# DFT over m and output projection in one-bank operations of 512 elements, in a re-searched order

## The chip, the cores and the metric

The program runs on one core of a Trainium2 chip. Its time is the device time of one execution in microseconds. The kernel before took 454.33 us (median of three runs, 454.22 to 454.91). The profile was taken on a further execution of 453.94 us, whose span from the first to the last instruction is 452.2 us.

Names used below: PE is the matrix engine, PEld its weight loads, DVE the vector engine, ACT the scalar engine, POOL the engine that cannot read PSUM, SP the queue that issues the transfers. PSUM is the memory that PE writes; it has eight banks of 512 fp32 numbers per partition here.

## What is computed

Four sequences of 6272 steps with 256 channels go through a gated recurrence and then through a gated long convolution:

```python
f = lower_bound + (1 - lower_bound) * sigmoid(f_logit)
h[t] = f[t] * h[t-1] + (1 - f[t]) * x[t]                 # recurrence, x becomes h
x1, x2, x3 = split(h @ w_proj)                           # 256 -> 3 * 256
conv = irfft(rfft(x2, n=S) * rfft(filter_fft, n=S), n=S) # over the sequence, S = 6272
out = (x1 * conv * x3) @ w_out
```

## The kernel before

The sequence is written as 6272 = 128 x 49, and the Fourier transform over it is done as small matrix products in two steps: one over m (128 values) and one over r (49 values). For each of the four batches there are these operations, each a short run of instructions recorded by `op` (L78) with what it reads and writes:

- `hgrn` (L342): 13 chunks. Loads of f_logit and x, a sigmoid on ACT ("sig"), a product on POOL ("u"), transposes on PE ("su", L374), the gate ("f", L387 on ACT or L389 on DVE) and the recurrence as a scan on DVE (L395). ("wrap" copies a part of h on POOL.)
- `gate` (L410): "x13" on PE (L423), one bank each; its results leave PSUM as "xs" copies on ACT or DVE, or as a product on DVE (L444); the rest of the products ("z") are on POOL (L453).
- `phase_p` (L720): the projection of x2, 13 operations "P" on PE (L729), with evictions "x2" of 1024 elements. P needs all scans of its batch.
- `phase_f1` (L737): the DFT over m. 16 operations "F1" of eight matmuls (L742), each into two banks, and each with one eviction "A" of 1024 elements into the buffer A, which has four slots of eight pairs.
- `unit` (L788): the DFT over r ("F2", L804), the product with the filter's spectrum (on DVE straight from PSUM, L827; or an ACT or DVE copy of 512 elements and then a POOL product, L836), the inverse over r ("I2", L846) and its eviction "Th" (784 elements).
- `phase_o` (L896): 13 groups of four rows (the last has one). "I1" (L909, two banks), the product "y" on DVE (L915) into one of two `ys` buffers, the output projection "proj" (L927: eight matmuls into two banks), one eviction "o" of 1024 elements into a staging buffer (`osb`, `PP` or `HA`, by `places`, L893), and one store. The first y of a batch needs all of the batch's I2 results and gate products.

A "y" begins only when its batch's spectrum is done; meanwhile the next batch's `hgrn` runs. So a batch has a first stretch (P, F1, F2, I2, x13, and some scans of the next batch) and a second one (I1, y, proj, o, and the last scans of the next batch).

The order of all of this is fixed in the kernel: `ORDER` (L126) is a text in which three characters give one operation, the engine that does it and its first PSUM bank. `emit` (L109) writes the operations out in this order, so that every engine has its own fixed queue. An operation that may run on two engines has its engine from there too ("MUL" is DVE's product straight from PSUM). `copy` (L286) writes an eviction for the engine it is given; the page shows these under L289 and L291 (ACT), L294 and L296 (DVE).

The buffer marks that set the dependences are `At` (L268, one mark for a slot of A), `Ax` (L272) and `place_t` (L887, the marks of a staging buffer).

Of the kernel before, what the change touches and what calls it, by code (L numbers as in the profile page):

```python
# [62 lines left out]
class Plan:  # L63
# [67 lines left out]
    "QD/WCPSERACSACQCD9MCNUEHQCOECUSEAOEBOCYWEcgEzgEngEogEIIEJIE0gELUE9gCVCCMYCTYESYCZGE1ACaSCbCCfWCgGEMMENMChQCiIETSEpAE"
    "eYCcYCjYEqYCdWEXUCeGCoQEYEEUKEVKCkWEZMCpAClGEfSE/ACvQCqUEjWEgKCwIEhKCrEEkGCxQErUCyIElOCtSFHgAGgFJAEvQEsEEtME+gCWgFIg"
    "FRgCuCAHgFSgFbgC4WEwAExIEKYE2YCsYAIYAJYAKYCzYE3SFAYC6UC5GE4CC7EFKYC8YAMYC0WE5KE6QC1GC/UE7IDBSFTADAMDCCE8IFBWC9UFESFC"
    "GC+EFDOFFCCHgFcgFlgB3gFmgFvgFwgDIQDJADKUDLEDEWDFGALIEWYAOYDDYDMYFUYDyYFLQFOUFGKFPEDPSFMIFNIDQCFdAFQMDaWDNSDOCDbGFeYA"
    "NYFVQFYUFZEFnAFWIFXIDRSJSWJTXFfQJUGDSCJVHFxAFaMJXWFiSFgIJZOFhIFjCDUUDVEFkKFoYFpWDhQEmYDTYEiYEuYFyYD2YEOYECYEaYD+YFsU"
    "DfSFqGFrODiADYQFtEDgCDZAFuMFzWDkSF0GF2QEyADdUCGgB2gC3gDeEDlCC2gMXgDHgG2gCXgMWgF5gCmgMigDXgCngF+gDcYDjYJWYMYAF6YF7YMZ"
    "YGkgDmgMvgDngMjgDGgDWgMugGtgG/gF1OJYWJcXF3IJeHF4IGMQGCUGISGJCJauGNIGDMGQQGGWGHOGUSGYUGVKGRAGOQGKWGPIMkAGZEGLGGEUGFEG"
    "ASGSWGWUGBKGTGJdSJhTJiWJfqGXEGaUGbEJjLJkuGcQGdAGgSGhKGeWJmUJnVGfGF8QJoMJpNGlSGuWGiUF9AGpqGyGG3QGjMJrXJsTG5AGnqGwuJbY"
    "GqYJqYJtHHIUJwXJxQGxYGmYJuDGzYGoYGvYJyHJzoGrSG7oHJEHAWG0UGsCG1EHOSHPCJ1RJ2QHKUHEuG4YJvYG6YG8YHBYMlYHFYJ3JHCuHLEJ6XHM"
    "SJ7RJ8PJ4oJ9pHNCG9UHTWG+EHSgHDYHQSJ/QHGUKARHbgHkgHtgHXGKBAHRKMwAHVuKCpHcSHHEHlWHnGKERHeqHgqH2UHWYHdYKFWKJSKGBHfYHUYH"  # L140
    "YYHhYHZQKHuHpuH3EKLCHiUHuSHaAHjEKKWHyqKMGH4QHwqH5AH6UH8WH9GKOTKQDHoYHxYHvYHmYJ+YMxYKNYHzYHqYH7MHrQIBWHsAH+UMaSIAgIDu"
    "IJgIFGH/MISgIbgIKQMeWMbCIOAMcKMfGH0UKPRH1EMgOIkSIEYKRpIMoIGYITUILYKDYICYIHWIVsM6gIugIlCIXEIIGKTRKVBMmSMnCIPYINYIUYIY"
    "YIWYIcWIgOMoKMqQIeGMrAIQUIREIZWKUSImUKYTMsIIvQM8AKWqKaLIaGIoWInEIqSKZUKdVIxoIzoKfNKbsJ0YIhYKXYIfYKSYIdYIpGIiWIrCIjGM"
    "yQIsSItKMzAM2WM7gMVgI3gNGgNHgKeUKiVKjSKnTJAgNSgNTgNfgNogORgNegJJgNIAM9YMdYJlYM0IM3GKgsKkFI4QM4OKpDM+UI6AKoTM/EKlqNCW"
    "KqrI8AKsSNDGNAMKuCNEOKhYJBQKtTKxSJgYIwYI5YIyYKvrJFANUAI0YNJYI1UJDoJEYI7YKzCI2EKwYKyRK0pK1YI9YKmYNKWNOSI+UNVYJCYKIYJL"
    "YJGYNLGNPCNMOK2RK3QI/EJKUNQKK7WK8XK4BNgAJMEK9GK5oNWSNaQJOsLAWK+vNXCNbANYKKrYJPYLCGNhYNcIKcYJNYJHUJIELBXLFWLDvLHGNiSL"
    "GULKWLIsNlQNjCNkKNqALMGLLXJQUNmALNvNnILPWLQSR1TR2XNpgU5gOagF/gOQgU6gNzgNygJREN9gN8gLUULRGR4HR3DN0ALSqLOYLJYLTYMhYM5Y"
    "K6YNrYK/YNFYLEYN1YM1YJ5YLVMLZQNsWNvSNwCNtGLWULaILbQLXELjUNxKNuOOGgOHgLYgObgLcALkMN2SLeWN5QLlULfONRYNNYN+AN/YLgWN3CN6"
    "ALmEOIALhGN4KN7ILoSLpKOAULtQODWLqSOBEOcAOSAOEGLrCLuIMtYNZYLvQLwAOJYOdYOTYNdYOCML3UOFOL4MLySOKWONQLdgLigL5ULzKL0SOLGO"
    "MOOOAU7AOPIL8WL6EL9OL1COUUR6QOVEOWMR8AOXSOeWOhQOYCOZKL+UOfGOiAOgOOjIL7gLsgVRgL/EVSgOkgVFgMGSMBWL2gLxgLngMAgMpYMHKMCO"  # L150
    "OlYOmYU8YNBYOrQOtUOzSO9WOuEOsIO0KO+GOvQO/UOpSOxWVTAOwIPAMOyGO7QO8IOqCVHAO3UOnWOoGO1QO2IO4EO5SMDWO6CMLQMEGMMIPBSPFUPC"
    "CMIWPGMMQSPLQMRKMJGPPoPNoPDUPEEPHSPICMNWR7RR9pPbUPJSPTQMFgMOGPKKPrWPdEPVoPXoPWYVUYPOYPYYPMYR5YPQYPUYPRSR/USAQSCIPfsP"
    "eYPsGPcYPSCPtWPjSPZQPnqSBEPuGPlCPvWPkYPgYPmYPaAPhUPwGPiMMKgP1gP2QSETSGDPxWP6oP4oVGgP+gQHgQQgQjgSDYPoYPyGPpUU9SPzWU+C"
    "PqEP0OSFRSJQSLAP/WQDGSHpU/KQZUSKQSORMSSSPXQaESMoP3YQAYQBuQCYMTCP7YQEYP5YSQBSRHVBUQISQKCP8QSTSVCMVDMQFWQRUP9ASVCQMqQG"
    "GQbQQcAQVsSUTQdWSWrQTsQUYSSYQNYQJYQLYSYSQeGVIYQWYVAYQSYQfQQgASZTSdVSfFQOWQhQVdgQsgSaKSbrQiIQkUVegQ1gQ+gQosQmsRRgQPGV"
    "fAQtSQvCQXWQYGSeQSiVSjSSgoSkFSlqVJWQxCQ2UVKGQpYQuYScYQlYVNQQ4MQwYSIYQyYQnYQ6EVLOQqSVOAVVUQrCVPIRHWVWEQzSRIGVXMQ/QQ0C"
    "RNWRDoRBoROGSnUSoVRJSSpERCYQ5YREYQ7YRAYRLWSsUQ3YStRVpgVqgRagMPgU4gV1gRjgSqtSuMSvpVgYRKCRMGQ8SRPWRQORSUVZQQ9CRWERkWVa"
    "ARUsRTYRXYRVYRmGVhSVbIVrAViCRFUV2gWLgWMgWBgWCgRsgRGMSxWSyQS2RSzGRoGRYUVjKS4BRZERbWS0oVlSVmCRduS3QS7RS8UTAWTBVS5oVnKS"
    "9BS+sV3ATCGTDtS1YVsYVtQVxSRnYRlYRpYRcYSrYS/YV4YSwYVuARfGVvITFUTGWTKXTLVTHERgYReYVyCTIuTPUTQQVzKTMHTURRqWTNtTREWDARrG"
    "TSoV5SRtUV6KV7KV9WTWBTVRTZQRxEV+GTaVTeSTfTTXpTbARhQTctV/OWNATgCRiAThrRvsTjVTkSToWTpXTlFTmqWEYR+YTqGTrHWFQTtWWGASXYRy"  # L160
    "YRwYRuYTsYRzUTvGWHITuXTyWTzSR0ETwvT0GT3UT1qT8QWIWaYSaZTWzgW9gW+gWVgVEYWOYS6YWWgW0gMUgWfgW1AWXAWJGT2YWYYTEYTiYTYYVwYT"
    "OYSmYTdYVMYSNYTTYTnYVYYTxYTJYShYT4MabDaaCT5UT9IWKOUBQT6EWPSWSWUCIWQCT+UWRKUGQWZSWTGT/EUHIWaCWhAUDUWUOUIQWbKUEEUJAULW"
    "UQUWcSUVQUMOUNWWggWpgWdCWqgT7gUFgUAgdcgWrAW/AUOGURMUSUUTEWeKUWIUaSV0YWiYWsYWAYVkYVQYW2YWjWWmQV8YVcYXAYWtUUbKWkGWnAVo"
    "YWlOUcSWoIWuEUXWWvMUfQUgIUdCUYGWwSW3UW6WWxCWyKW4EUhQW5MW7GW8OddgUiAadSXBUXEQXCEXDMUKgUUgdogUZgd0gdpgUegd1gUPgXHgUpWU"
    "kUXFAXGIXSQafCXaSdeAXbCUlMUqOXgUXYWXMSXhEXTIXWUXNKXXMXZGXOWXPGdqAUmSXiUUnKXUWXeQXQSXVOXfIXjEd2AXKWXRCXLGXcUXdEUogUjg"
    "UzSUuQdfYUrWUvIU0KdrYXIYXJYd3YUsGXmUacYXnMXoQXkSXqWXpAXrGaeUUwQagEXlKXsWXtOUxAXuSdgUXwqXyCX2WdhEaiQajTanSaoRX6uakAX4"
    "GahYXxYalrapCdkWaqBXvYX3YXzYX5YX7YdlGasQdiMX0SauAdmOYOUX+QYCIYAoX1CYPEdsSYGWdtCYIGX8UYKuX/YYBYarYatRaxWayQavpYLYYDYY"
    "YgeAgYJYeBgYqgYhgX9EYSUduKazGa0AYEWYZQYdoYTEYFGYQUYREa2SYUWa3Ta7Ra4Ka5rYeYYboY8UYHYa1YYcYYVGYWSYXKdwWa9BY9EeCAa8RbAQ"
    "bBSbDCbCAYMUYiSdxOa+pdyOYmqYNEYkCYaYYnYbEYa/YYlYYjYd4QbFWd5AbHGd6Id8Ud9Ed+MYfSYrWYgCYtGY+QYoSY0UY/AYzgUtgZGgeMgeYgZP"
    "gYvuY4sY2sY5YYsYYuYY3YeDYY1YYwYYpCZCQZDAeZgZYgZhgeNgZAWbGSbKTbIqZBGbMDYxQZEWZHUYyAZFOZLsZQSY6WZUqZJEbLUeEQbNsZSCY7GZ"  # L170
# [23 lines left out]
def kernel(  # L194
# [542 lines left out]
    def phase_f1(b, u):  # L737
        def mm(e, pb):
            pa = PS[:, pb:pb + 2].rearrange("m a (i c) -> m (a i) c", c=128)
            for i in range(UE):  # L740
# [1 line left out]
                nc.tensor.matmul(pa[:, i, :], X2[:, j:j + 128], D1, start=True, stop=True)  # L742
# [270 lines left out]
```

## Time and profile before

| | us |
|---|---|
| median of three runs | 454.33 |
| the profiled execution, its own time | 453.94 |
| its span, first to last instruction | 452.2 |
| PE busy | 436.2 (96%) |
| DVE busy | 407.1 (90%) |
| ACT busy | 391.1 (86%) |
| POOL busy | 317.6 (70%) |

The page gives for each engine the time in which it had an instruction in flight. Instructions overlap: the mean of one, times their count, is more than the busy time of the group. For PE the overlap is large, and a busy PE is not a PE at its peak. The chain of waits follows the work that ended last backwards, at each step to what released it. The view by windows gives the busy time of each engine between two moments.

### The profile page before, as it was taken

To read this page: it belongs to the slowest core of one execution; us is meant where nothing else is said; L and a number is where in the kernel's file an instruction comes from. 1 tells how busy PE (TensorE), PEld (TensorE's weight loads), DVE (VectorE), ACT (ScalarE), POOL (GpSimd) and SP (SyncE) were. 2 spreads that over 40 slices of the span, in tenths; PEclk is the share of its full clock that TensorE was granted. 3 is DMA by queue.
4 is the path that set the end of the run, shared out by engine and by line. 5 is a ranking of instruction groups with operands and counts; after the bars stand their busy time and mean duration, and the time that the engine had idled before them with its cause. 6 is when DMAs were issued, how large, how long until landed. Compare 5 with 4: busy or idle time off the path is not lost.

```text
span 452.2 us, 14532 instructions
## 1 busy us (share of the span) xinstructions
PE 436.2 (96%) x6013; PEld 345.1 (76%) x6013; DVE 407.1 (90%) x459; ACT 391.1 (86%) x539; POOL 317.6 (70%) x301
## 2 busy tenths in 40 slices
PE   8899999999999999999999999999999999999994
PEld 7787768777667889767768989777769897766783
DVE  8799998799999997999999987999999948989774
ACT  6679999899999968999999869999988979987553
POOL 6578998289999942678997828969996805676400
PEclk9999999999999999999999999999999999999998
DMA  8999999657998475777966992598946613763167
GB/s 330 407 368 334 404 368 367 253 187 249 371 356 308 191 230 229 240 255 244 410 249 189 323 319 106 199 327 307 386 161 236 269 71 107 225 235 102 49 268 304
DMA packets 42563, 119.05 MB, mean 263 GB/s; under 512 B 4096, under 2 KB 5760, under 8 KB 42496
## 3 DMA queue, kind: packets, MB, share of 16 engines
q1 hardware_dynamic: 42496, 118.11, 71.9%
q8 instruction: 47, 0.77, 0.7%
q14 instruction: 20, 0.16, 0.1%
...
## 4 chain that ended last, share of the span: by engine, by line
PE 74%; DVE 13%; DMA 4%; issue 3%; ACT 3%; POOL 1%; SPq 0%; DVEq 0%; ACTq 0%; POOLq 0%
PE PS L423 18%; PE PS L846 10%; PE PS L729 10%; PE PS L927 7%; PE PS L374 7%; PE PS L804 7%; DVE HA L395 7%; PE PS L742 6%; DVE ys L915 4%; PE PS L909 3%; PE PS L666 3%; DMA HA<-in_moe_filter_fft_dram 3%; DMA X<-in_moe_filter_fft_dram 1%; PE PS L684 1%; POOL PP L836 1%
## 5 line engine op out<-in xcount | busy, mean ns | idle before, releaser
L395 DVE TENSOR_TENSOR_SCAN HA<-fTs,HA,PS 128x512 f16<-128x512 f32 (+1 forms) x96 | 112.5, 1201 | 1.3 <-ACT fTs L387 0.6
L423 PE MATMUL PS<-HA,W 128*128 128x490 f16 (+1 forms) x416 | 102.1, 367 | 0.1
L836 POOL TENSOR_TENSOR PP<-HA,Hu 98x1008 f16<-98x1008 f16 x46 | 96.4, 2104 | 4.8 <-ACT HA L289 2.8
L289 ACT CAST HA<-PS 128x1024 f16<-128x1024 f32 (+1 forms) x107 | 85.0, 824 | 4.4 <-PE PS L742 2.4
L362 POOL TENSOR_TENSOR XT<-XT,FL 128x1024 f32<-128x1024 f32 (+1 forms) x31 | 67.0, 2165 | 20.1 <-ACT FL L360 20.0
L915 DVE TENSOR_TENSOR ys<-PS,zt 128x1024 fp32r<-128x1024 f32 (+1 forms) x52 | 58.4, 1152 | 10.4 <-PE PS L909 6.9
L387 ACT ACTIVATE fTs<-PS,nomc 128x512 f32<-128x512 f32 (+1 forms) x88 | 57.9, 669 | 7.2 <-PE PS L374 2.0
L927 PE MATMUL PS<-Wo,ys 128*128 128x256 f32 x392 | 57.6, 293 | 3.7 <-DVE ys L915 2.8
L444 DVE TENSOR_TENSOR zt<-PS,XS 128x490 f16<-128x490 f32 (+1 forms) x88 | 55.9, 649 | 5.6 <-PE PS L423 3.4
L827 DVE TENSOR_TENSOR PP<-PS,Hu 98x1008 f16<-98x1008 f32 x50 | 59.0, 1198 | 1.2 <-PE PS L804 0.7
L846 PEld LDWEIGHTS <-PP 98*128 98x128 f16 x1024 | 49.7, 97 | 11.2 <-POOL PP L809 2.0
L362 POOL TENSOR_TENSOR X<-X 128x1024 f32<-128x1024 f32 x21 | 50.0, 2382 | 9.6 <-ACT X L360 7.4
L846 PE MATMUL PS<-FT,PP 98*128 98x98 f16 x1024 | 55.7, 206 | 0.4 <-POOL PP L809 0.2
L927 PEld LDWEIGHTS PS<-Wo,ys 128*128 128x128 f32 x392 | 49.4, 188 | 8.4 <-DVE ys L915 2.6
L423 PEld LDWEIGHTS <-W 128*128 128x128 f16 x416 | 34.7, 97 | 27.7 <-issue 3.6
L289 ACT CAST Th<-PS 128x784 f16<-128x784 f32 x61 | 49.8, 819 | 5.6 <-PE PS L846 4.8
L291 ACT ACTIVATE XS<-PS 128x490 f32<-128x490 f32 (+1 forms) x84 | 48.5, 579 | 4.1 <-PE PS L423 1.9
L729 PE MATMUL PS<-W,HA 128*128 128x256 f16 x392 | 43.8, 273 | 0.1
L729 PEld LDWEIGHTS <-HA 128*128 128x128 f16 x392 | 42.9, 142 | 0.5
...
L289 ACT CAST X<-PS 128x1024 f16<-128x1024 f32 (+1 forms) x32 | 31.8, 1054 | 10.1 <-PE PS L729 9.7
L804 PE MATMUL PS<-HA,FT 64*128 64x256 f16 x512 | 38.0, 271 | 0.5 <-ACT Hm L291 0.2
...
## 6 DMA issues: line engine op xcount, KB each, us to landing
...
```

Of the source, the lines that this page charges most:

```text
L289: nc.scalar.copy(dst, src)
L362: op("u", {"POOL": 0.1 + 0.553 * nb}, lambda e, xt=xt, ft=ft: nc.gpsimd.tensor_tensor(xt, xt, ft, op=AOP.mult), r=[("ft", k)], w=[("xt", k)])
L387: nc.scalar.activation(fT, sT, AF.Identity, scale=by, bias=1.0)
L395: nc.vector.tensor_tensor_scan(h, fT, bank(pb)[:, 512 - hn:512 + hn], init, op0=AOP.mult, op1=AOP.add),
L423: nc.tensor.matmul(PS[:, p, 0:n], W13[:, kh, js], HA[:, HB[kh] + t0:HB[kh] + t0 + n], start=(kh == 0), stop=(kh == 1))
L729: nc.tensor.matmul(pp[:, r - r0, :], column(HB[kh], q_of(r)), W2[:, kh, :], start=(kh == 0), stop=(kh == 1))
L804: nc.tensor.matmul(PS[:, xb + e2, :].rearrange("p (i k) -> p i k", k=64)[:, :, ks], FT(rows, o, r), A[rows, ka:ka + UE, r, ks], start=(r = ...
L827: nc.vector.tensor_tensor(pr, px.unsqueeze(1).broadcast_to([TB, 2, UE, 63]), hh(), op=AOP.mult)
L836: nc.gpsimd.tensor_tensor(pr, spec[:, o, :, 1:64].unsqueeze(1).broadcast_to([TB, 2, UE, 63]), hh(), op=AOP.mult)
L846: nc.tensor.matmul(PS[:, ib + o, pr * TB:(pr + 1) * TB], PP[:TB, k, o, n, 2 * pr:2 * pr + 2, :], v[:TB], start=(n == 0), stop=(n == 1))
L915: nc.vector.tensor_tensor(late["ys"][:, yk, :, 0:rn * 128], PS[:, cb:cb + 2, 0:rn * 128], late["zt"][:].rearrange("p k r m -> p k (r m)") ...
L927: nc.tensor.matmul(po[:, i, :], late["ys"][:, yk, kh, i * 128:(i + 1) * 128], Wo[:, kh, :], start=(kh == 0), stop=(kh == 1))
```

## The change

F1 becomes two operations of four matmuls, each into one bank, with an eviction of 512 elements each; the marks `At` and `Ax` are then kept by halves of a slot of A. The output projection becomes two operations of two rows (four matmuls, one bank) with an eviction of 512 elements each; the staging buffers' marks are kept by halves. A store still carries four rows and waits for both halves. The number of matmuls and of transfers stays the same.

```diff
     def At(u):
-        return [("At", u % NA)]
+        return [("At", u % NA, o) for o in range(2)]
...
     def phase_f1(b, u):
-        def mm(e, pb):
-            pa = PS[:, pb:pb + 2].rearrange("m a (i c) -> m (a i) c", c=128)
-            for i in range(UE):
-                j = (u * UE + i) * PW
-                nc.tensor.matmul(pa[:, i, :], X2[:, j:j + 128], D1, start=True, stop=True)
-        f1 = op("F1", {"PE": 0.056 * UE}, mm, r=[("x2", g) for g in range(NX2)] + ["D1", "padX"], take=2)
-        k = u % NA * UE
-        op("A", either(1024), lambda e, pb: copy(
-            e, A[:, k:k + UE],
-            PS[:, pb:pb + 2].rearrange("p a (i r k) -> p (a i) r k", r=2, k=64)),
-           w=At(u) + Ax(u), src=f1)
+        for h in range(2):
+            hn = UE // 2
+
+            def mm(e, pb, h=h):
+                for i in range(hn):
+                    j = (u * UE + h * hn + i) * PW
+                    nc.tensor.matmul(PS[:, pb, i * 128:i * 128 + 128], X2[:, j:j + 128], D1, start=True, stop=True)
+            f1 = op("F1", {"PE": 0.056 * hn}, mm, r=[("x2", g) for g in range(NX2)] + ["D1", "padX"], take=1)
+            k = u % NA * UE + h * hn
+            op("A", either(512), lambda e, pb, k=k: copy(
+                e, A[:, k:k + hn],
+                PS[:, pb].rearrange("p (i r k) -> p i r k", r=2, k=64)),
+               w=[At(u)[h], Ax(u)[h]], src=f1)
...
     def phase_o(b):
...
-            po = op("proj", {"PE": 0.259 * rn}, proj, r=[("y", yk)], take=2)
-            at, kt = places[g], place_t(*places[g])
...
-            op("o", either(256 * rn), stage, w=kt, src=po)
+            at = places[g]
+            kt = place_t(*at, 0) + (place_t(*at, 1) if rn > 2 else [])
+            for j in range(0, rn, 2):
+                jn = min(2, rn - j)
+
+                def proj(e, ob, yk=yk, j=j, jn=jn):
+                    for i in range(jn):
+                        for kh in range(2):
+                            nc.tensor.matmul(PS[:, ob, i * 256:i * 256 + 256],
+                                             late["ys"][:, yk, kh, (j + i) * 128:(j + i + 1) * 128],
+                                             Wo[:, kh, :], start=(kh == 0), stop=(kh == 1))
+                po = op("proj", {"PE": 0.259 * jn}, proj, r=[("y", yk)], take=1)
+
+                def stage(e, ob, at=at, rn=rn, j=j, jn=jn):
+                    v = place(*at)
+                    to = v[:, j // 2] if at[0] == "z" else v[:, j:j + jn]
+                    copy(e, to, PS[:, ob, 0:jn * 256].rearrange("m (r e) -> m r e", e=256), OS)
+                op("o", either(256 * jn), stage, w=place_t(*at, j // 2), src=po)
```

The text `ORDER` is another one throughout. Read out, it gives these counts (all four batches):

| operation | before | after |
|---|---|---|
| F1 on PE | 64 | 128 |
| proj on PE | 52 | 100 |
| eviction A | ACT 58, DVE 6 (1024 each) | ACT 110, DVE 18 (512 each) |
| eviction o, without the four of one row | ACT 46, DVE 2 (1024 each) | ACT 84, DVE 12 (512 each) |
| spectrum product straight on DVE / by copy and POOL | 74 / 54 | 68 / 60 |
| gate product straight on DVE / by copy and POOL | 88 / 16 | 96 / 8 |
| eviction x2 | ACT 32, DVE 20 | ACT 30, DVE 22 |

The order of the large steps on PE (the place of P, of the first I1 and of the last scan's transposes in each batch) is the same in both; the order is another one inside these steps. Some small operations of the setup change their engine too.

More of the change, by code (lines that the diff above doesn't have):

```diff
@@ L131 @@
[L131 to L170, printed above, removed]
@@ L186 @@
[L186 to L189 removed]
+    "AAYAPYA0gA4gAiQAdQAkQAzAAWYABIACIADIAbQAcQAQIATIAeQA1YAgQA2QAhSA8gBIgBAgBEgA5YA6SAfUApUA9IA7KAjUAmUAsUA+UBFIBBYA3AAR"
@@ new lines @@
+    "AASAAoSBCSAUYBJYAtQBGQBMgDogBQgBYgA/EBHAAXIBUgBcgBggBkgDrgDsgEPgD3gAEgD4gEDgDqgEEgDpgEbgAxWEQgEcgEngAlWBKWAZUArVBNYB"
+    "RIBSQBZIBDCBLGBTAAnVBOSAvVBaWBVIBWQBdIBPCBbGBXABhIAqVAyVAuVBeSBiWBlYAwVBjGAaEDtABfKDuYBmQBnIBoWBpOBqUBrEAVIAYABxQBvW"
+    "ByIBtUBwOERAB6QB4WDvSBuMD5ABsYB5OB7AAFYBzYB8YD6YB0UB1EDwKDxKDzWD0OD1OB9QB+ACIUCKSCBQCJEEFAD7UB/WD8ECLKCCICNSD/QD9MCA"
+    "GEAIEBIEGYCOCCEWCRUEdACDYCMYEHSESYCSEEIKEJKCFGCaUCbECYQCZAELWEpAEeYEzgEogCPUCQEEMOENOEKYCTYCcYEqYETSEUCEVKE9gE+gCdQC"
+    "eACUUCoWCqQCfSE1AE/ACpOCrICVECgKEXWChQEfSEYOEZOCiAEgCCtUCuEEhKCkQClAAHgE0gFHgEjWErUAGgFRgEsEEkOElOFAYCjYCsYE2YC6SC7C"
@@ new lines @@
+    "FJACxQEvSCvWEwCCwGCyIEtMC4QE3UC0WExKC5AFTAC1GE6QDBSFBWAJYEiYE7AAIYCzYE4ME5MCHgFIgFbgFSgCXgCGgFcgFlgFmgE8IDCCFCGC/UDA"
+    "EC9SC+CFdAALYAKYFKYC8YAMYDDYFUYFEQCmgFwgFvgDEUFDODIWFLSFFIFGIDJGDFEFMKFNKDKWDLGFOQDRUFPAFQIDSEDMYFeYFnAFVWFoYEuYDNSD"
+    "OCFYUFWOFXODaQFfSFZEFaMDbAFgCDPWJyQJzRFxADQGFiUFhKAOIFjMFkMJ0AJ1BDUWDVGFpSFyYDhQANYDTYEOYEmYEaYDyYFsWFqCDfUDiAEyYD2Y"
+    "EWYD+YECYDYQFrKFtGDgEFzSDZAF0CFuOJ3UJ4VF2WF1KDkQDdSB3gB2gDGgNOgC3gNPgF5gCWgC2gNagNbgG+gNQADlADeCCngDmgNmgDngF+gDXgGs"
+    "gDWgDHgHHgJ2YF6YF7YDcYF3OJ5MF4OG1gJ8UJ6tGQWJ+EGRGGEQGMUGFAGNEGWWGAQGXOGKUGYWGCSGBANcAGZGGLMGIQGUUGGWNoAGDKGJIGOSGVMG"
@@ L190 @@
+    "nhYnwYl5EmBWoAToBSf5UmCGoFWoCLoDqoEYoGOoaSoMQf6Ef9goTUoJWoHXoNIoQQoORoKGoIHoUMobKohWoXUoYEoVVoWFoiOovSoRAoPJocUoeVof"
+    "NodEojQokAolRomBowKooUo2Wo9QoLgopMozSoxToyDoqUosVo0KorEotFo+Io3OpLSoZgpBUo/Vo6Qo4RoSgpEWpMKpFOpCEpAFo7Ao5BoggongpNQp"
+    "PRo1gpISpGTougpQBpHDo8gpOIpJKpRgpKgpDgpSQpZWpTIpUTpWSpXCpVLpaOpYgpbTpcLpdg"
 )
@@ L885, in rows_of, with place_t @@
         return v, a.rearrange("p (j r) e -> p j r e", j=2)
-    def place_t(kind, i):
-        return {"p": lambda: [(t, i, o) for t in ("P", "Pz") for o in range(2)],
-                "a": lambda: [t for j in (2 * i, 2 * i + 1) for t in At(j) + Ax(j)],
-                "z": lambda: [("zr", i)], "o": lambda: [("osb", i)]}[kind]()
+    def place_t(kind, i, h):
+        return {"p": lambda: [(t, i, h) for t in ("P", "Pz")],
+                "a": lambda: At(2 * i + h) + Ax(2 * i + h),
+                "z": lambda: [("zr", i, h)], "o": lambda: [("osb", i, h)]}[kind]()
     places = (("o", 0), ("o", 1), ("p", 0), ("p", 1), ("a", 0), ("a", 1), ("o", 0),
@@ L921, in phase_o @@
                w=[("y", yk)], src=i1)
-            def proj(e, ob, yk=yk, rn=rn):
-                po = PS[:, ob:ob + 2].rearrange("m a (r e) -> m (a r) e", e=256)
-                for i in range(rn):
-                    for kh in range(2):
-                        nc.tensor.matmul(po[:, i, :], late["ys"][:, yk, kh, i * 128:(i + 1) * 128],
-                                         Wo[:, kh, :],
-                                         start=(kh == 0), stop=(kh == 1))
-            po = op("proj", {"PE": 0.259 * rn}, proj, r=[("y", yk)], take=2)
-            at, kt = places[g], place_t(*places[g])
-            def stage(e, ob, at=at, rn=rn):
-                to, of = rows_of(*at, PS[:, ob:ob + 2].rearrange("m a (r e) -> m (a r) e", e=256), rn)
-                copy(e, to, of, OS)
+            at = places[g]
[14 more added lines that the diff above has]
+                op("o", either(256 * jn), stage, w=place_t(*at, j // 2), src=po)
             def leave(e, at=at, r0=r0, rn=rn):
```

78 lines of the change are left out of this document (55 added, 23 removed).

## The prediction

> **What bounds the kernel now.** I read the page's first part and its chain of waits, then the windows cut at the first "y" of each batch, then the groups by shape, and last the timeline of the end.
>
> ```profile
> span 452.2 us, 14532 instructions
> ...
> PE 436.2 (96%) x6013; PEld 345.1 (76%) x6013; DVE 407.1 (90%) x459; ACT 391.1 (86%) x539; POOL 317.6 (70%) x301
> ...
> PE 74%; DVE 13%; DMA 4%; issue 3%; ACT 3%; POOL 1%; SPq 0%; DVEq 0%; ACTq 0%; POOLq 0%
> ```
>
> PE carries three quarters of the chain, but 13% of it (59 us) runs through DVE. The stretches show why (columns: length, then busy us and count of PE, PEld, DVE, ACT, POOL, granted clock, DMA share, GB/s):
>
> ```profile
> 0.00:70.60 70.60, 65.43 (x740) 52.39 (x741) 64.34 (x85) 59.61 (x81) 56.64 (x78) 1.00 0.98 370
> 70.60:142.70 72.10, 71.29 (x992) 53.63 (x992) 66.86 (x77) 67.95 (x96) 58.39 (x51) 1.00 0.84 297
> 142.70:239.30 96.60, 95.65 (x1412) 75.83 (x1408) 91.99 (x98) 87.61 (x124) 71.17 (x60) 1.00 0.70 252
> 239.30:337.90 98.60, 97.37 (x1420) 76.73 (x1416) 92.45 (x100) 89.73 (x128) 78.42 (x65) 1.00 0.75 265
> 337.90:425.67 87.77, 86.82 (x1207) 69.41 (x1207) 75.10 (x87) 75.08 (x102) 53.04 (x51) 1.00 0.46 161
> 425.67:452.20 26.53, 19.62 (x270) 17.10 (x264) 16.40 (x15) 11.06 (x12) 0.00 (x0) 0.94 0.66 263
> ...
> 142.30:165.40 23.10, 22.21 (x402) 19.47 (x398) 22.87 (x22) 20.93 (x30) 19.92 (x19) 1.00 0.57 209
> ```
>
> I call the first six rows stretches 1 to 6: the setup, then from the first P, then from the first y of batch 0, 1, 2 and 3. In stretches 3 and 4 DVE is busy for 95% and 94% and ACT for 91% of the time; within stretch 3 the part in which y and scans alternate (last row) has DVE at 99%. Three engines are thus nearly full in the middle of the kernel, and an edit that gives DVE and ACT more to do isn't free there.
>
> **The price of a split eviction.** Means of one instruction, by shape:
>
> ```profile
> L289 ACT CAST HA<-PS 128x1024 f16<-128x1024 f32 x58 | 57.4, 1022 | 3.2 <-PE PS L742 2.4
> L291 ACT ACTIVATE osb<-PS 128x1024 f32<-128x1024 f32 x24 | 24.2, 1027 | 11.1 <-PE PS L927 11.0
> L289 ACT CAST afs<-PS 128x512 fp32r<-128x512 f32 x21 | 11.9, 592 | 0.6 <-PE PS L666 0.5
> L294 DVE CAST HA<-PS 128x1024 f16<-128x1024 f32 x6 | 7.2, 1220 | 0.6 <-PE PS L742 0.5
> L294 DVE CAST afs<-PS 128x512 fp32r<-128x512 f32 x11 | 7.2, 681 | 1.0 <-PE PS L666 1.0
> L827 DVE TENSOR_TENSOR PP<-PS,Hu 98x1008 f16<-98x1008 f32 x50 | 59.0, 1198 | 1.2 <-PE PS L804 0.7 <-ACT XS L291 0.2 <-ACT HA L289 0.2
> L444 DVE TENSOR_TENSOR zt<-PS,XS 128x490 f16<-128x490 f32 x81 | 52.1, 658 | 4.5 <-PE PS L423 2.5 <-ACT XS L291 1.1
> L291 ACT ACTIVATE XS<-PS 128x490 f32<-128x490 f32 x77 | 45.1, 587 | 4.1 <-PE PS L423 1.9 <-PE PS L846 1.4 <-DVE Th L294 0.4
> L289 ACT CAST Th<-PS 128x784 f16<-128x784 f32 x61 | 49.8, 819 | 5.6 <-PE PS L846 4.8
> ```
>
> Two halves against one whole are 2 x 0.592 - 1.022 = +0.16 us on ACT and 2 x 0.681 - 1.220 = +0.14 us on DVE. But instructions in a row overlap:
>
> ```profile
> 85.05 1.94 ACT HA L289 x2
> ...
> 23.61 2.48 DVE L294 CAST afs<-PS 128x512 fp32r<-128x512 f32 x4 [0.99 <-PE PS L666]
> ```
>
> The second of two whole ACT evictions adds 1.94 - 1.02 = 0.92 us, so about 0.1 is hidden; four half DVE evictions take 0.60 each after the first. I therefore take 0.08 us off every ACT mean and 0.06 off every DVE mean. Summed with the counts of the order before, that gives 88.6 (ACT) and 91.6 (DVE) for stretch 3, where the rows above say 87.61 and 91.99: good enough to carry over. So a split costs about 0.08 us (0.16 at most), and the 112 splits 9 us (17 at most), on two engines together.
>
> [...]
>
> **Where the load lands.** I cut the order after at the same marks (first P, first y of each batch) and priced the difference of counts.
>
> - Stretch 1: DVE -0.5 us, ACT +3.1, POOL -5.5 (small setup work moved). Its DVE work from the first to the last scan grows by 0.7. The loads set its beginning: 0, between -0.5 and +0.7.
> - Stretch 2: DVE -1.4, ACT -0.4: two direct products (1.14 each) and two copies of x1 or x3 fewer on DVE, three more half evictions. Neither engine is alone the bound: between -1.4 and 0, I take -0.7.
> - Stretch 3: ACT does 32 half A evictions instead of 15 whole ones (32 x 0.51 - 15 x 0.94 = +2.2), 22 half o for 13 whole (-1.0), two more x2 (+1.9), three more xs (+1.5), and one more spectrum copy, Th and sigmoid (+2.3): +7 us. DVE has 3 less. ACT then needs 87.6 + 7 = 94.6 to 95 of 96.6 us, 98%. What waits behind a late ACT is PE: F2 for A, I1 for Th, the gate for xs. No stretch here shows an engine over 95.2% (DVE in this one). At 95.2% the stretch is 95/0.952 = 99.7, +3.1; at a full ACT it is 0. I take +2.3, nearer the share that a row shows.
> - Stretch 4: DVE has two more x2 (+2.3), three more direct gate products (+1.8), a copy more (+0.6), five half A for two whole (+0.7), one o less (-0.9), one direct product less (-1.1): +3.4, so 95.9 of 98.6 (97%). At 95.2% that is 100.7, +2.1; at full use 0. I take +1.5 by the same reason. ACT has 2 less.
> - Stretch 5: DVE +4.9 to 80.0 of 87.8, ACT -3.0 to 72: room on both, 0.
> - POOL gets six more products of 2.1 us and loses eight of 1.15. Its heaviest stretch is then 4 with 79.5 of 98.6: hidden.
> - The y-and-scan parts have the same 9 or 10 y's and 12 or 13 scans on DVE in both orders: 0.
> - Transfers and matmuls are the same in number; a store waits for its second half, and nothing but a later store to the same place waits for it: 0.
>
> **PE's own side.** A change between operations on 64 rows (su, F2, mini, I1) and those on 128 rows happens 230 times in the order before and 242 times in the one after; 57 more PE instructions have a wait. The idle time before weight loads that nothing else explains:
>
> ```profile
> PEld L804 <- issue: 4.4, 12, 0.4
> ...
> PEld L423 <- issue: 3.6, 17, 0.4
> ...
> PEld L742 <- issue: 3.1, 14, 0.4
> ```
>
> Spread over 230 changes these 11.1 us are 0.05 each, so 12 more cost 0.6; at 11.1/43 = 0.26 each, where they show, it is 3.1. With 0.2 for the waits I take +0.8 (0 to +3.3).
>
> **The end.** In the tail there is nothing but I1, y, proj and o, and here splitting should help. DVE's rows after its first two y's:
>
> ```profile
> 428.19 2.36 DVE L915 TENSOR_TENSOR ys<-PS,zt 128x1024 fp32r<-128x1024 f32 x2 [0.17 <-PE PS L927]
> 431.13 1.23 DVE L915 TENSOR_TENSOR ys<-PS,zt 128x1024 fp32r<-128x1024 f32 x1 [0.58 <-PE PS L927]
> 434.07 2.35 DVE L915 TENSOR_TENSOR ys<-PS,zt 128x1024 fp32r<-128x1024 f32 x2 [1.71 <-ACT PP L291]
> ...
> 444.65 1.23 DVE L915 TENSOR_TENSOR ys<-PS,zt 128x1024 fp32r<-128x1024 f32 x1 [0.86 <-PE PS L909]
> 447.39 0.43 DVE L915 TENSOR_TENSOR ys<-PS,zt 128x256 fp32r<-128x256 f32 x1 [1.52 <-PE PS L909]
> 448.53 0.42 DVE L296 TENSOR_SCALAR osb<-PS 128x256 f32<-128x256 f32 x1 [0.71 <-PE PS L927]
> ```
>
> From the first y (425.67) to the last eviction's end (448.95) are 23.3 us, 16.4 of them DVE work and 6.9 idle. The idle 1.71 ends with ACT's whole eviction: an I1 waited for its two banks. After, six half o's stand on DVE (6 x 0.60 for the one whole of 1.13): 18.9 us of work. Walking the new order with a y at 1.15, a half proj at 0.47, a half o at 0.51 or 0.60 and an I1 at 0.5, I find some 2 us of idle left (before the y of group 9, of group 11, and the last two steps), so 21 against 23.3. I take -1.9, between -3 and 0.
>
> **Sum.** 453.94 (the profiled execution; 452.2 of span and 1.7 around it) + 0 - 0.7 + 2.3 + 1.5 + 0 + 0.8 - 1.9 = 455.9. That is 0.35% over the median of 454.33.
>
> **Rivals.** (1) Banks come free sooner and PE waits less: faster. A whole A eviction holds two banks for 1.02 us after its matmuls, a half one bank for 0.59, and 13% of the chain on DVE leaves something to gain. The price is bounded by the engines: stretch 3 cannot be shorter than ACT's 95 (-1.7) nor stretch 4 than DVE's 95.9 (-2.7). Half of these 4.4, with the stretch 2, PE and end terms as above: 453.94 - 2.2 - 0.7 + 0.8 - 1.9 = 449.9. It decides if ACT is over 98.3% busy in stretch 3 or DVE over 97.3% in stretch 4; against it, no row shows that over 90 us, for it, 99% was held for 23 us. [...]
> (2) The shares stay at 95.2%, the changes of row mode cost their upper price, and the end gives nothing: 453.94 + 3.1 + 2.1 + 3.3 - 0.7 = 461.7; with the end at -1.9, 459.8. [...]
> (3) Load and relief cancel: 453.4 to 455.2, no change. For it: the totals of ACT and DVE grow by only 1 to 1.5%, and the large steps stand where they stood.
>
> **How the numbers follow.** Forecast 455.9, with a range of its own from 455.2 to 458.5: 0.36. Rival 1: 0.34. Rival 3: 0.16. Rival 2: 0.14. About 0.2%, 0.9 us, is what a measurement tells from no change. So faster 0.34, same 0.16, slower 0.50. The range reaches to 448.5 below (rival 1 with a little more than half of its bound) and to 461.5 above (rival 2), with 0.2 outside.
>
> **What would show it.** Right: ACT at 95 to 97% from the first y of batch 0 to that of batch 1, and that stretch 2 to 3 us longer; the next one 1 to 2 us longer with DVE at 95 to 96%; DVE's idle time after the last batch's first y at 2 to 4 us instead of 6.9, and the time from there to the end 1 to 2 us shorter; half evictions at 0.58 to 0.60 (ACT) and 0.68 us (DVE). Wrong: stretches 3 and 4 at or under 96.6 and 98.6 us with engines over 97% (rival 1), or the end as long as before. If the first P comes over 1 us earlier or later than 70.6 us after the first instruction's start (before: stretch 1 ends there), the setup's moved work mattered, which I put at nothing.

## The result and the profile after

The changed kernel took 455.61 us (median of 22 runs, 454.52 to 456.83) beside 454.51 us for the kernel before on the same chip (22 runs, 454.18 to 455.72). The ratio is 1.0025, with an interval of 1.0016 to 1.0033. The profiled execution of the changed kernel took 454.52 us, with a span of 452.6 us; it is the quickest of the 22. The kernel before has 453.94 and 452.2 in its profiled execution, so the two profiles differ by 0.6 us where the medians differ by 1.1.

From the page after, the engines and the shares of the chain of waits:

```profile
PE 436.6 (96%) x6013; PEld 346.4 (77%) x6013; DVE 412.7 (91%) x488; ACT 392.6 (87%) x631; POOL 317.9 (70%) x290
...
PE 68%; DVE 13%; issue 5%; ACT 5%; DMA 4%; POOL 3%; SPq 0%; DVEq 0%; ACTq 0%; POOLq 0%
```

ACT runs 92 instructions more than before and is busy for only 1.5 us more; DVE runs 29 more for 5.6 us. PE's share of the chain falls from 74% to 68%, and the difference goes to several waits, with no new large one. None of POOL's instructions reads PSUM in either profile (301 before, 290 after); that it cannot, as the list of names has it, no run tried. That alone doesn't tell where the time went, so the stretches are cut again, after and before, at the first P matmul and at the first y of each batch (columns as in the prediction: length, then busy us and count of PE, PEld, DVE, ACT, POOL, clock, DMA share, GB/s). After:

```profile
0.00:73.17 73.17, 66.55 (x744) 52.73 (x744) 64.55 (x94) 64.49 (x85) 53.99 (x70) 1.00 0.97 362
73.17:144.14 70.97, 70.57 (x989) 53.28 (x989) 65.29 (x77) 66.62 (x109) 58.63 (x48) 1.00 0.79 277
144.14:240.95 96.81, 95.89 (x1404) 76.36 (x1403) 88.75 (x97) 90.49 (x153) 73.03 (x61) 1.00 0.77 274
240.95:339.99 99.04, 97.04 (x1442) 77.65 (x1438) 95.56 (x107) 89.05 (x149) 77.36 (x63) 1.00 0.70 253
339.99:427.19 87.20, 86.84 (x1184) 69.10 (x1178) 79.76 (x96) 72.07 (x121) 54.85 (x51) 1.00 0.47 163
427.19:452.60 25.41, 19.74 (x278) 17.31 (x274) 18.77 (x20) 9.91 (x18) 0.00 (x0) 0.94 0.69 275
```

Before, with the cut at the first P matmul, which stands at 71.41 in its timeline (the prediction cut 0.8 us earlier):

```profile
71.41:142.70 71.29, 70.48 (x987) 53.21 (x987) 66.16 (x76) 67.22 (x96) 57.58 (x48) 1.00 0.83 296
```

| stretch | before, us | after, us | difference | predicted |
|---|---|---|---|---|
| 1, to the first P | 71.41 | 73.17 | +1.76 | 0 |
| 2, to the first y of batch 0 | 71.29 | 70.97 | -0.32 | -0.7 |
| 3, to that of batch 1 | 96.6 | 96.81 | +0.2 | +2.3 |
| 4, to that of batch 2 | 98.6 | 99.04 | +0.4 | +1.5 |
| 5, to that of batch 3 | 87.8 | 87.20 | -0.6 | 0 |
| 6, to the end | 26.53 | 25.41 | -1.12 | -1.9 |

The profiled execution loses 1.8 us ahead of the first P and wins some 1.4 us back behind it. The timeline of the changed kernel shows what happens there (columns: start, length of the run, engine, line, operation, tiles, count; in brackets the idle time before it and what ended it). PE:

```profile
22.79 2.34 PE L672 MATMUL PS<-D1r,f 128*128 128x256 f32 x16 [0.79 <-DVE f L300]
27.00 0.73 PE L690 MATMUL PS<-afs,FTr 64*128 64x512 f32 x4 [1.88 <-DVE FTr L302]
...
73.17 10.86 PE L735 MATMUL PS<-W,HA 128*128 128x256 f16 x98
```

PE does the first transforms of the filter (FF1, L672), is done at 25.13, and waits 1.88 us for the second (FF2, L690), which reads the table FTr. Its releaser is DVE. The same stretch of DVE's and POOL's timelines:

```profile
24.25 2.61 DVE L302 TENSOR_SCALAR FTr<-HA,cols 128x196 fp32r<-128x196 f32 x2
...
24.20 2.35 POOL L368 TENSOR_TENSOR XT<-XT,FL 128x1024 f32<-128x1024 f32 x1 [3.37 <-ACT FL L366]
```

and the groups by shape:

```profile
L302 DVE TENSOR_SCALAR FTr<-HA,cols 128x196 fp32r<-128x196 f32 x1 | 2.4, 2431 | 0.0
L302 DVE TENSOR_SCALAR FTr<-HA,cols 128x98 fp32r<-128x98 f32 x1 | 0.3, 259 | 0.0
```

The larger of the two instructions has twice the elements of the smaller, and lasts nine times as long. It starts 0.04 us after POOL's first product ("u"), and ends 0.12 us after it. Before, POOL wrote this table, ahead of its first product, and FF2 followed FF1 with no wait:

```profile
21.42 1.30 POOL L303 TENSOR_SCALAR FTr<-HA,cols 128x196 fp32r<-128x196 f32 x2
...
25.05 0.73 PE L684 MATMUL PS<-afs,FTr 64*128 64x512 f32 x4
```

This is one of the "small operations of the setup" that change their engine in the new order (operation "tabs", function `f_tables`). It has nothing to do with the splitting of the evictions.

A second thing isn't in the profiled execution. The executions of the changed kernel come in two groups: with a granted clock of 0.995 to 0.997 they take 454.5 to 455.4 us (one, at 0.999, 455.8), with 0.992 to 0.994 they take 455.8 to 456.8. The kernel before is at 0.995 or above in all 63 of its runs whose clock is on record. The experiments below tell whether this has the same cause.

### The profile page after: what moved, and what is told of

The parts are those of the page before. It is cut to its first block, busy times and chain, and to the rows that moved or that the text cites. A ratio compares the mean times of both kernels' runs of the same rounds, so it can differ in the third digit from the quotient of the medians.

```text
span 452.6 us, 14678 instructions
## 1 busy us (share of the span) xinstructions
PE 436.6 (96%) x6013; PEld 346.4 (77%) x6013; DVE 412.7 (91%) x488; ACT 392.6 (87%) x631; POOL 317.9 (70%) x290
## 4 chain that ended last, share of the span: by engine, by line
PE 68%; DVE 13%; issue 5%; ACT 5%; DMA 4%; POOL 3%; SPq 0%; DVEq 0%; ACTq 0%; POOLq 0%
PE PS L429 17%; PE PS L939 9%; PE PS L854 9%; PE PS L735 8%; PE PS L750 7%; PE PS L812 6%; PE PS L380 6%; DVE HA L401 6%; PE PS L917 4%; DVE ys L923 3%; DMA HA<-in_moe_filter_fft_dram 2%; DVE fTs L395 2%; ACT X L295 2%; DMA X<-in_moe_filter_fft_dram 1%; ACT HA L295 1%
## 5 line engine op out<-in xcount | busy, mean ns | idle before, releaser
L844 POOL TENSOR_TENSOR PP<-HA,Hu 98x1008 f16<-98x1008 f16 x51 | 107.1, 2108 | 6.0 <-ACT HA L295 2.9
L295 ACT CAST HA<-PS 128x512 f16<-128x512 f32 (+1 forms) x163 | 88.7, 605 | 4.9 <-PE PS L750 1.4
L939 PE MATMUL PS<-Wo,ys 128*128 128x256 f32 x392 | 60.6, 296 | 3.3 <-DVE ys L923 2.6
L450 DVE TENSOR_TENSOR zt<-PS,XS 128x490 f16<-128x490 f32 (+1 forms) x96 | 60.8, 649 | 2.3 <-ACT XS L297 0.8
L295 ACT CAST Th<-PS 128x784 f16<-128x784 f32 x63 | 51.9, 826 | 5.2 <-PE PS L854 3.6
L835 DVE TENSOR_TENSOR PP<-PS,Hu 98x1008 f16<-98x1008 f32 x45 | 53.7, 1198 | 2.1 <-PE PS L812 0.9
L750 PEld LDWEIGHTS <-X 128*128 128x128 f16 x512 | 32.1, 98 | 12.0 <-issue 3.7
L295 ACT CAST X<-PS 128x1024 f16<-128x1024 f32 (+1 forms) x30 | 30.0, 1074 | 12.9 <-PE PS L735 12.9
L750 PE MATMUL PS<-D,X 128*128 128x128 f16 x512 | 40.2, 219 | 0.4 <-DVE PP L835 0.2
```

What stands on the lines that cost most here:

```text
L295: nc.scalar.copy(dst, src)
L450: nc.vector.tensor_tensor(zd(), px, xs(0), op=AOP.mult)
L750: nc.tensor.matmul(PS[:, pb, i * 128:i * 128 + 128], X2[:, j:j + 128], D1, start=True, stop=True)
L844: nc.gpsimd.tensor_tensor(pr, spec[:, o, :, 1:64].unsqueeze(1).broadcast_to([TB, 2, UE, 63]), hh(), op=AOP.mult)
L939: nc.tensor.matmul(PS[:, ob, i * 256:i * 256 + 256], late["ys"][:, yk, kh, (j + i) * 128:(j + i + 1) * 128], Wo[:, kh, :], start=(kh == 0) ...
```

## The experiments

### Is it the setup? (setup_old, setup_new)

The first question was whether the order ahead of the first P makes the loss. Each kernel takes that part of `ORDER` from the other one. In both, one gate eviction at the seam, the place where the two orders meet, reads another PSUM bank than its matmul wrote, so a part of h's gate is computed from other data; the work is the same in kind and number.

```diff
 # setup_old: ORDER of after, ahead of the first P of batch 0 in the sequence of before; among it
-(tabs FTr, DVE)   behind the second afs
+(tabs FTr, POOL)  ahead of the first u
 # setup_new: ORDER of before, ahead of the first P of batch 0 in the sequence of after; among it
-(tabs FTr, POOL)  ahead of the first u
+(tabs FTr, DVE)   behind the second afs
```

> The kernel after, with the order, engines and banks of the kernel before for all operations ahead of the first P of batch 0 (the setup), the rest in the new order. In the profiles the first P starts at 73.2 us after the change and at 71.6 before. Setup theory: the first P is back at 71.6 to 72.0 and the 1.6 us stay won to the end: 454.0 (453.6 to 454.4), at or under the kernel before. Rival, that the new order's middle is bound by ACT and DVE load and not by its start: what is won in the setup is lost again by the first y of batch 1, 455.3 to 455.8.

> The kernel before, with the setup's order, engines and banks of the kernel after; whole evictions as before. Setup theory: the first P comes 1.6 us later and the end too: 456.0 (455.4 to 456.4). Rival, that the setup doesn't matter: 454.5 (454.2 to 454.8).

setup_old took 457.58 us (5 runs, ratio 1.0078, 1.0065 to 1.0091), slower than either parent, and neither theory had that. Its timeline of PE, and its window there:

```profile
71.69 0.60 PE L735 MATMUL PS<-W,HA 128*128 128x256 f16 x4
74.36 12.09 PE L735 MATMUL PS<-W,HA 128*128 128x256 f16 x94 [2.08 <-ACT XS L297]
```

```profile
75.00:80.00 5.00, 5.00 (x33) 4.20 (x32) 0.55 (x1) 3.03 (x3) 2.30 (x3) 0.66 0.97 308
```

P begins at 71.69, where the setup theory had it, but after four matmuls PE stops for 2.08 us: at the seam, P waits for a gate copy on ACT, which the first P of neither parent does. Right behind the gap the clock is 0.66 over 5 us. Its time says nothing of the setup, then, since the graft brought a wait of its own; but it shows a PE gap of some 2 us followed by a lower clock.

setup_new took 457.98 us (5 runs, ratio 1.0071, 1.0057 to 1.0084), a larger loss than either theory expected, but in the direction of the setup theory:

```profile
25.00:30.00 5.00, 3.10 (x16) 2.28 (x14) 4.54 (x5) 2.93 (x5) 2.55 (x5) 0.76 1.02 410
30.00:35.00 5.00, 4.89 (x68) 4.04 (x68) 4.29 (x5) 3.24 (x5) 2.55 (x2) 0.90 0.89 306
```

PE is idle for 1.9 us of the first window, waiting for FTr on DVE, and the clock is 0.76 and 0.90 in the two. Its first P stands at 75.04: 3.6 us later than before. The wait is 1.9 of that, and the lost clock 5 x 0.24 + 5 x 0.10 = 1.7.

### The splits by themselves (f1_split, proj_split, both_split)

Each keeps the order of before and puts two halves in the place of each whole, on the same engine and in the same two banks: f1_split the F1 part of the change's diff, proj_split the `phase_o` part, both_split both.

```diff
 # f1_split, in ORDER
-F1 (PE, bank b), A (engine e)
+F1 (PE, bank b), F1 (PE, bank b + 1), A (engine e, bank b), A (engine e, bank b + 1)
 # proj_split, in ORDER
-proj (PE, bank b), o (engine e)
+proj (PE, bank b), proj (PE, bank b + 1), o (engine e, bank b), o (engine e, bank b + 1)
 # both_split: both
```

> The kernel before with only F1 and its eviction A split into halves, each pair in place of the whole one, same engine, neighbouring banks, old order elsewhere. Load theory: 64 splits at 0.08 us are 5 us of ACT and DVE, spread over four batches whose engines are 91 to 95 percent busy, so about a third shows: 456.0 (455.3 to 457.0). Relief theory, that banks freed sooner let PE go on: 453.5 (452.5 to 454.2).

> The kernel before with only proj and its eviction o split into halves in place, old order elsewhere. Relief theory: in the tail the banks come free sooner, idle time of DVE there falls from 6.9 us by 0.5 to 1.5, elsewhere DVE is the bound and nothing changes: 453.5 (453.0 to 454.0). Load theory: 46 splits on ACT at 0.08 are 3.7 us, half of it seen: 456 (455 to 457).

> The kernel before with both splits in place (F1 with A, proj with o), old order, old engines. If the two effects seen alone add (454.05 and 453.91 against 454.35): 453.6 (453.2 to 454.0). If the 9 us of added ACT and DVE work begin to show once both are there: 454.5 to 456.

f1_split took 454.05 us (11 runs) and proj_split 453.91 (11 runs) beside 454.35 for the kernel before: ratios 0.9992 (0.9983 to 1.0001) and 0.9988 (0.9979 to 0.9996). both_split took 454.03 (11 runs) beside 454.24: 0.9995 (0.9986 to 1.0003). Each split alone lies in the range of its relief theory, and both together lie just outside the range that the sum of the two was given (453.2 to 454.0). So the load theory is out, and a relief of more than a few tenths too: the splits themselves change the time by about -0.2 us, within what a measurement can tell from none (only proj_split's interval leaves out 1).

The page of both_split, its windows for stretches 3 and 6, and a line of DVE's timeline at the end:

```profile
PE 436.2 (96%) x6013; PEld 344.8 (76%) x6013; DVE 407.8 (90%) x467; ACT 394.9 (87%) x643; POOL 317.4 (70%) x301
```

```profile
143.04:239.57 96.53, 95.69 (x1412) 75.89 (x1408) 91.92 (x99) 88.92 (x151) 71.15 (x60) 1.00 0.70 252
...
425.98:452.30 26.32, 19.42 (x260) 16.71 (x253) 16.47 (x16) 11.56 (x22) 0.00 (x0) 0.92 0.67 266
```

```profile
434.17 2.36 DVE L923 TENSOR_TENSOR ys<-PS,zt 128x1024 fp32r<-128x1024 f32 x2 [1.55 <-PE PS L939]
```

104 more ACT instructions make ACT busy for 3.8 us more (394.9 for 391.1): 0.037 each. Eight more on DVE cost 0.7 us: 0.09 each. In stretch 3 ACT has 27 instructions more than before, is busy for 1.3 us more, and the stretch is as long as before. The end is hardly shorter either: 26.32 for 26.53. The idle time of DVE before the y's at 434 is 1.55 us there, for 1.71 before. So the splits alone don't shorten the end. In the changed kernel, whose order also gives DVE six of the half o's there, it is 25.41; whether those or another part of the order make it so wasn't tried.

### The table back, or earlier (tables_pool, tables_early, old_tables_dve)

Here a single entry of `ORDER` moves. Three characters are an entry: "AVI" is `f_tables` on DVE, "AVY" the same on POOL.

```diff
 # tables_pool, from after: on POOL, ahead of the first u ("DuY")
-BfKDuY
+BfKAVYDuY
...
-BrEAVIAYA
+BrEAYA
 # tables_early, from after: on DVE, some 5 us earlier
-BXABhI
+BXAAVIBhI
...
-BrEAVIAYA
+BrEAYA
 # old_tables_dve, from before: on DVE, behind the third afs ("ByK")
-EFAAVYBnI
+EFABnI
...
-ByKBwO
+ByKAVIBwO
```

> The kernel after with one operation moved: the scaling of the filter's tables FTr (two instructions) is on POOL ahead of its first product, as in the kernel before, instead of on DVE between the first evictions. In the profile after, the 196-element one lasts 2.43 us on DVE, and PE idles 1.88 us for it. Table theory: PE's idle goes, the first P starts at 71.5 to 72.0 instead of 73.2, the granted clock is the same in all runs (0.996 to 0.998), and both together give 452.9 (452.3 to 453.5), faster than before. Rival, that the middle of the new order loses the time: 455 to 456, with the clock still changing between runs.

> The kernel after with the same operation left on DVE, but some 6 us earlier, when POOL has no product running. Port theory, that DVE's instruction was held until POOL's product ended: the two instructions last 0.3 us each and the gain is that of POOL's version, 452.9 (452.3 to 453.5). Rival, that this instruction is slow on DVE by itself: it lasts 2.4 us again and delays DVE by 2 us, 454 to 455.5.

> The kernel before with that operation alone moved from POOL to DVE, behind its third eviction of the filter's transform, when POOL's first product has begun. Table theory: the instruction lasts 2 us or more, PE idles 2 to 2.8 us at 25 to 28 us, the clock drops in some runs (0.992 to 0.996), the time is 456.5 (455.5 to 458). Rival, that it takes its 0.6 us and the setup absorbs it: 454.3 to 454.9.

tables_pool took 452.77 us (10 runs, 452.39 to 454.48) beside 454.24 for the kernel before: 0.9971 (0.9962 to 0.9981). It beats both kernels. From its timeline, POOL and then PE:

```profile
20.61 1.31 POOL L309 TENSOR_SCALAR FTr<-HA,cols 128x196 fp32r<-128x196 f32 x2
...
70.97 10.86 PE L735 MATMUL PS<-W,HA 128*128 128x256 f16 x98
```

P comes 2.2 us earlier than after, and no run has a clock below 0.995. tables_early leaves the table on DVE, and takes 452.85 us (5 runs, 0.9967, 0.9955 to 0.9979), with P at 71.01. So DVE isn't the wrong engine for the table; the moment is wrong. It also settles another reading: in the waits of the changed kernel, the weight load ahead of the first FF2 is put down to an instruction of ACT (X, L366: 2.1 us). Here only the table has moved, and FF2 follows FF1 with no wait, at 24.90. The timeline and the groups of tables_early:

```profile
19.15 0.50 DVE L302 TENSOR_SCALAR FTr<-HA,cols 128x196 fp32r<-128x196 f32 x2
```

```profile
L302 DVE TENSOR_SCALAR FTr<-HA,cols 128x196 fp32r<-128x196 f32 x1 | 0.3, 318 | 0.0
L302 DVE TENSOR_SCALAR FTr<-HA,cols 128x98 fp32r<-128x98 f32 x1 | 0.3, 264 | 0.0
```

The instruction that lasts 2431 ns beside POOL's product lasts 318 ns without it. In the changed kernel it ends 0.12 us behind the product's end, and so it does in old_tables_dve below (2255 ns from 25.49, the product 2.35 us from 25.28), where it starts 0.21 us after the product and not 0.04. In the three other profiles that have it at this moment, the first FF2 waits for it too: 1.90 us in after_again and in setup_new, and 0.15 in filler, behind 1.92 us of idle matmuls. Not every DVE instruction is held like that. In tables_pool two evictions from PSUM run beside the same product of POOL, 1.35 us for both (before, such an eviction has a mean of 681 ns):

```profile
24.00 2.40 POOL L368 TENSOR_TENSOR XT<-XT,FL 128x1024 f32<-128x1024 f32 x1 [2.08 <-ACT FL L366]
...
24.28 1.35 DVE L300 CAST afs<-PS 128x512 fp32r<-128x512 f32 x2 [0.16 <-PE PS L672]
```

The traces thus have it at 2.43 us (after) and 2.26 (old_tables_dve) where POOL's 2.35 us product started first, each time ending just behind the product, and at 0.32 us where POOL was idle (tables_early, from 14.04 to 20.18 us): by its length and its end it is held until the product is over. What holds it, a port as in the name of the theory or something else, and why the two evictions are not held, no trace here shows.

old_tables_dve is the opposite test: the kernel before with this one operation moved to DVE. It took 458.98 us (5 runs, 1.0101, 1.0087 to 1.0114), more than the 458 at which the expected range ended. POOL's and DVE's timelines, then the waits of PE, then the windows:

```profile
25.28 2.35 POOL L362 TENSOR_TENSOR XT<-XT,FL 128x1024 f32<-128x1024 f32 x1
...
25.49 2.43 DVE L296 TENSOR_SCALAR FTr<-HA,cols 128x196 fp32r<-128x196 f32 x2
```

```profile
PE PS L684 <- DVE FTr L296: 2.8, 1, 2.8
```

```profile
25.00:30.00 5.00, 2.19 (x10) 1.37 (x9) 4.28 (x5) 1.06 (x1) 3.07 (x5) 0.71 1.02 417
30.00:35.00 5.00, 5.00 (x47) 4.15 (x47) 3.48 (x5) 1.71 (x3) 2.54 (x2) 0.61 0.24 97
```

The wait is back, 2.8 us of it, and the clock is at 0.71 and 0.61 in the windows around its end and behind it. One operation on the other engine, with all else unchanged, costs 4.7 us of 454.

### Is the lower clock a consequence of the gap? (filler, after_again)

filler is the changed kernel with 16 matmuls more, whose result nothing reads, between the FF1s and the first FF2: PE still waits for the table, but is busy meanwhile. after_again is the changed kernel itself, run beside it on the same chip.

```diff
-WARM = 24
+WARM = 28
 # in ORDER: four "warm" operations (four matmuls each) in bank 3 ahead of the first FF2
```

> The kernel after with four more operations of idle matmuls (16 of 128x256, results unused) on PE ahead of the first FF2, so that PE works during most of the 1.9 us in which it waits for DVE's table instruction. The wait itself stays. Clock theory, that the time lost besides the wait is the clock lowered because PE was idle: the granted clock is 0.996 or more in nearly all runs and the time is that of the best runs of the kernel after, 454.6 (454.2 to 455.0). Rival, that what changes from run to run is the wait's length or a late load: the time stays at 455.6 (455.2 to 456.2) with clocks from 0.992.

> The kernel after, unchanged, beside the one with idle matmuls on the same chip: 455.6 again (455.2 to 456.1), clocks from 0.992 to 0.997. In a profile with a clock under 0.995 the windows from 25 to 35 us show it lowered, and the first P later than the 73.2 us of the profile with 0.997. If the lowered clock is elsewhere, the table's wait is not its cause.

filler took 454.79 us (11 runs, 454.33 to 455.28), after_again 455.41 (10 runs, 454.57 to 456.58), beside 454.30 for the kernel before: ratios 1.0010 (1.0001 to 1.0019) and 1.0024 (1.0012 to 1.0035). PE in filler:

```profile
24.80 1.92 PE L624 MATMUL PS<-iden 128*128 128x256 f16 x16
26.88 0.73 PE L690 MATMUL PS<-afs,FTr 64*128 64x512 f32 x4 [0.15 <-DVE FTr L302]
```

FF2 comes no earlier than in the changed kernel (26.88 for 27.00), so the wait is still paid. But all eleven runs of filler have a clock of 0.995 or above, and none takes longer than 455.28. The ten runs of after_again fall in two halves: five at 0.996 to 0.997 with 454.57 to 454.88 us, five at 0.992 to 0.994 with 455.94 to 456.58. Its profiled execution is of the second kind:

```profile
25.00:30.00 5.00, 3.10 (x28) 2.39 (x28) 4.77 (x6) 2.73 (x4) 2.31 (x5) 0.83 1.01 406
30.00:35.00 5.00, 5.00 (x61) 3.98 (x58) 4.57 (x7) 3.44 (x4) 2.56 (x2) 0.83 0.86 307
```

Cut into single microseconds, the clock is full up to 28 us, 0.63 and 0.67 in the first and the last of the four after that, and half in the two between:

```profile
29.00:30.00 1.00, 1.00 (x16) 0.78 (x17) 0.77 (x2) 0.17 (x1) 0.00 (x0) 0.50 0.99 397
30.00:31.00 1.00, 1.00 (x12) 0.87 (x11) 0.64 (x2) 0.00 (x0) 0.72 (x2) 0.50 1.05 422
```

Over the four, 0.37 + 0.50 + 0.50 + 0.33 = 1.7 us of clock are lost, and this begins about a microsecond after PE has taken up its work again (27.05). Both its first P (74.35 for 73.17) and its median against the quicker half are 1.2 to 1.5 us later. So the gap has two prices: 1.9 us of waiting, in both profiled executions, and some 1.5 us of lower clock in about half of all executions (10 of 22, and 5 of 10).

The gap before it is 1.90 us long. In the profile of the changed kernel, with a gap of 1.88 us, the clock is 1.00 in every single microsecond from 24 to 36 us. So a gap of 1.9 us was enough for a lower clock in about half of the executions, and what sets these apart no run shows.

### What it adds up to

| step, each against the kernel before on its own chip | us |
|---|---|
| both splits in the old order (both_split) | -0.2 |
| with the new order as well, the table off DVE (tables_pool) | -1.5 |
| the table on DVE beside POOL's product, PE kept busy (filler) | +0.5 |
| the changed kernel (after_again) | +1.1 |

The new order without its table is worth 1.3 us, the wait for the table costs 2.0, and the lowered clock 0.6 in the median. What in the new order wins the 1.3 us wasn't tried; in the profile of the changed kernel it is the end (-1.1) and stretch 5 (-0.6) that are shorter.

## Why the prediction was right or wrong

The total was right: slower, 455.61 for 455.9, inside the forecast's own range. The way to it was not. Two terms that the sum didn't have, +1.8 in the setup and the lowered clock, took the place of a load that mostly didn't come. That the total fits is luck: with the table where it was, on POOL ahead of its first product, the same order is 1.5 us faster than the kernel before (tables_pool), and the sum would have been the same but for those 0.6 us of DVE's work in the setup.

**The setup, put at 0 ("the loads set its beginning").** This is the step that failed. I priced the moved setup work as busy time of each engine: DVE -0.5, ACT +3.1, POOL -5.5. The term was 0, between -0.5 and +0.7; it measured +1.76. In this sum the table is a saving on POOL and some 0.6 us on DVE (0.32 and 0.26 in tables_early). What counts is who waits for each moved operation and what runs beside it: FF2 waits for FTr, and POOL's product runs beside it. My own condition, the first P over 1 us late, was met: 73.17 for 71.41 (the 70.6 that I gave as the mark was not yet the first P).

**The clock.** No step spoke of it: the granted clock stood at 1.00 in every row I quoted but the last stretch's 0.94, and I never asked what a new gap on PE would do to it. It is worth 0.6 us of the 1.1.

**A split costs 0.08 us.** It costs 0.037 on ACT and 0.09 on DVE, by both_split's page: half of the price on ACT, the price itself on DVE. On ACT the duration of one instruction, even with 0.08 taken off, overstates what a further one adds to the engine's busy time. With 90 of the added instructions on ACT and 22 on DVE that is 90 x 0.037 + 22 x 0.09 = 5.3 us where the prediction had 9. The durations were right: 110 half A evictions on ACT have a mean of 609 ns and 18 on DVE of 684, as the groups after show:

```profile
L295 ACT CAST HA<-PS 128x512 f16<-128x512 f32 x110 | 60.0, 609 | 2.0 <-PE PS L750 1.4 <-POOL PP L844 0.3
...
L300 DVE CAST HA<-PS 128x512 f16<-128x512 f32 x18 | 11.9, 684 | 0.3 <-POOL PP L817 0.2
```

**Stretch 3, +2.3.** It is +0.2. ACT grew by 2.9 us to 90.5, not by 7 to 95, so the share of 98% that the term hung on never arose. The counts explain most of it. The groups of ACT in the two windows have 26 xs copies in both, where I counted three more, and 13 sigmoids for 14, where I counted one more: by the sum's own 0.5 and about 1 us for each, some 3.5 of the 4.1 us that are missing. The other counts came as I took them (32 half A, 22 o, 9 x2, one spectrum copy and one Th more).

**Stretch 4, +1.5.** The load was right: DVE 95.6 us for a predicted 95.9. The step from load to time was wrong: I held that an engine doesn't go past the 95.2% that a row showed, and DVE is at 95.56 of 99.04, 96.5%. The highest share seen in a profile is what was needed there, not what can be had. The stretch is 0.4 longer, the lower third of the term's range.

**Stretches 2 and 5.** -0.3 lies in the range of -1.4 to 0. In stretch 5 DVE is at 79.8 (predicted 80.0) and ACT at 72.1 (72), and the room that I saw there was real; that it would be 0.6 quicker I didn't see.

**PE's changes of row mode, +0.8.** Not seen. The idle time before weight loads that nothing else explains, the same three lines as before:

```profile
PEld L812 <- issue: 4.7, 12, 0.4
...
PEld L750 <- issue: 3.7, 15, 0.4
...
PEld L429 <- issue: 2.5, 11, 0.4
```

That is 10.9 us where it was 11.1, with 12 more changes. That the changes make this idle time, which the term took as given, no run tried.

**The end, -1.9.** It is -1.1. The splitting itself, which I thought would help here, doesn't: with both splits in the old order DVE's idle time in the tail is 6.7 us (6.9 before). Right was what the new order does there: six half o's on DVE, and 18.8 us of DVE's work as predicted (18.9). From the first y at 427.19 to the last eviction's end at 449.69 are 22.5 us, so the idle time is 3.7, inside my 2 to 4 but not the 2 that the sum used:

```profile
435.25 2.36 DVE L923 TENSOR_TENSOR ys<-PS,zt 128x1024 fp32r<-128x1024 f32 x2 [0.21 <-PE PS L939]
...
447.65 0.69 DVE L302 TENSOR_SCALAR osb<-PS 128x512 f32<-128x512 f32 x1 [0.95 <-PE PS L939]
449.27 0.42 DVE L302 TENSOR_SCALAR osb<-PS 128x256 f32<-128x256 f32 x1 [0.59 <-PE PS L939]
```

The idle 1.71 before the y's at 434 is gone (0.21 at 435.25). What I walked through too smoothly are the last steps, where DVE waits for proj before each o.

**The rivals.** That the engines stay at their share and PE pays in full (rival 2) is out. No change (rival 3) is what the splits alone give: both_split is at 454.03. Whether a relief pays for their load there, or the engines had room for it, isn't shown. That banks come free sooner (rival 1) has no support as a mechanism, since neither split gains more than 0.12%, and the shares that it needed, ACT over 98.3% in stretch 3 or DVE over 97.3% in stretch 4, weren't reached (93.5% and 96.5%); but its sign is that of the change without the table, 452.77.
